# Longer runs for broadcast codes, six keys to a partition, and later loads in a routed attention kernel

## The chip, the core and the metric

The kernel runs on one core of a Trainium2 chip. The core has a matrix engine (TensorE, PE in the profile; its weight loads are PEld), a vector engine (VectorE, DVE), an activation engine (ScalarE, ACT), a general engine (GpSimd, POOL) and a queue engine (SyncE, SP), which here only issues DMA transfers. Each engine works through its own instructions in order, and waits on semaphores where it needs another one's result. Transfers run on 16 DMA engines, which all queues share. The metric is the device time of one execution in microseconds (us); lower is better.

## What is computed

Two blocks follow each other: an attention in which each query sees only the keys of its own cluster, and a two-layer network with the activation h - tanh(h).

```python
# attention: 4 batches, 8 heads, 768 positions, head size 64, 16 clusters
q_assign = np.argmax(np.einsum('bhsd,hcd->bhsc', q_n, c_n), axis=-1)
k_assign = np.argmax(np.einsum('bhsd,hcd->bhsc', k_n, c_n), axis=-1)
mask = q_assign[:, :, :, None] == k_assign[:, :, None, :]
scores = scale * np.matmul(q, k.transpose(0, 1, 3, 2))
scores = np.where(mask, scores, -1000000000.0)
...
attn = attn / (np.sum(attn, axis=-1, keepdims=True) + 1e-09)
return np.matmul(attn, v).astype(np.float32)
# network: 3072 tokens, width 512, inner width 2048
h = x @ w_in
g = h - np.tanh(h)
return (g @ w_out).astype(np.float32)
```

The n in q_n, k_n and c_n stands for normalised vectors. The order of the keys of a head plays no part in the result, so long as k and v have the same one.

## The kernel before

**Pairs and steps.** Two heads make a pair, and there are 16 pairs: four to a batch. Pairs 0 to 3 are batch 0. The attention of a pair has two halves of 384 queries, and a half has three steps of 2 x 128 keys. The list of steps (L1055) first has half 0 of pairs 0 to 3 (12 steps), then half 1 of pairs 0 to 3 (12 steps), and then pairs 4 to 15 with six steps each. One loop (L1204) goes through the steps and writes out, for each, the instructions of all engines in the order in which they are to run; nothing is reordered later. In a step, the scores of the following step are begun (`begin`, L473), the values of the present one are multiplied (`value`, L529), and a list of small jobs, `todo`, is spread between the matmuls of the network's work that fills the step.

**Codes and masks.** `load` (L317) fetches q and k of a pair on SP's queue; `turn` transposes them, on PE for batch 0 and on DVE in blocks of 32 for the others. `similar`, `turn_back`, `route` and `route_on` (L368 to L407) find the cluster of every query and key, as a number, the code. `publish` (L418) transposes the codes on PE, copies them to SBUF as bfloat16 (L427) and stores them to DRAM (L429), from where they are broadcast over partitions.

There are two ways to apply the mask. For half 0 of pairs 1 to 3 (the function `masked`), `spread_both` (L441) broadcasts the codes of queries and keys of each head to 64 partitions, into a tile named hot. `one_hot` (L452) turns them on DVE into a 0/1 row per cluster for the queries and a large negative number for the keys, in two instructions (L456, L460). A small matmul (L492) then adds the product to the scores before the exponential (L503). In all other halves, `spread` (L433) broadcasts the query codes to 128 partitions, into a tile named row, and `select` (L505) compares and multiplies on DVE (L513).

In `codes` a number stands at [partition, query or key, block of 128, head], and in DRAM in the order side, half, block, head, position. So one head's codes lie in runs of 128 numbers.

**When things are due.** `before` (L1059) yields the stages of a pair's preparation, and a table, `ready` (L1082), tells the step of each: for pairs of batch 0 the steps 0 to 4 after 3 (n - 2), for the others the steps -1, 0, 1 and 3 after a first step that is the pair before's first. The first stage of a pair n of batches 1 to 3 is its turn (of k; the turn of q has a place of its own, TURN_Q), and right behind it stands the load of pair n + 1:

```python
            def turns():
                turn(n, 1, nc.scalar)
                if rowwise(n):
                    turn(n, 0, nc.scalar)
                if n >= HP:
                    load(n + 1)
```

**The network.** The first half of batch 0 is multiplied plainly (L710, L726). From the second half on it is done with seven products in place of eight blocks. `up_items` (L881) gives a list of products for each of eight row blocks i, in the order 1, 2, 6, 7, 4, 5, 3. Products 6, 4 and 5 multiply differences of the input (the tile diff, made on DVE by `right_factors`, L879), the others the input itself. Their PSUM results (pu, L913) rotate through three buffers that other small results share, and DVE adds them (L908). Their weights come in as a stream from DRAM (`fetch_factors`, L833), two blocks ahead, in three buffers. The combined weights are made on DVE in steps 20 to 23 and stored by SP (L775). `start_without` (L950) takes a list of products and puts the first two of the second block ahead of the third of the first one; the half batch of batch 0 and the last batch use it.

**Queues.** SP issues nearly all transfers, in the order in which the program writes them. POOL issues the loads of the network's weights (raw, L218), which ACT and DVE then round (L149, L158, L161), as many pieces in each step as a table of paces says.

Of the kernel before, what the change touches and what calls it, by code (L numbers as in the profile page):

```python
# [30 lines left out]
F32 = mybir.dt.float32  # L31
# [8 lines left out]
P = 128  # L40
# [18 lines left out]
def kernel(  # L59
# [119 lines left out]
    def fast():  # L179
# [133 lines left out]
        def rowwise(n: int):  # L313

            return n < HP

        def load(n: int, what=(0, 1)):  # L317
            if n >= len(pairs):
                return
            b, p = pairs[n]  # L320
            for i in what:
                if i < 2:
                    pool, tag = (gp, "g") if b == 0 else (loads, f"x{i}")
                    shape = [P, NCH, 2, D] if rowwise(n) else [P, NBL, BL]
                    t = raw_qk[n, i] = pool.tile(shape, F32, name=f"x{i}", tag=tag)
                else:
                    pool = vp0 if n in (2, 3) else vp
                    t = vals[n] = pool.tile([P, 2, NCH, D], F32, name="vals")
                for h in range(2):
                    src = (q, k, v)[i][b, 2 * p + h]  # L330
                    if i == 2 or rowwise(n):
                        nc.sync.dma_start(
                            t[:, :, h] if i < 2 else t[:, h],
                            src.rearrange("(j p) d -> p j d", p=P),
                        )
                        continue
# [81 lines left out]
        def publish(n: int):  # L418

            sides = 2 if masked(n, 0) else 1  # L420
            G = HCH * 4 * sides
            ps = ps_f.tile([G, P], F32, name="pq", tag="f")
            nc.tensor.transpose(
                out=ps, in_=codes[n][:, 0:sides].rearrange("p i j h -> p (i j h)"), identity=ident
            )
            t = rtp.tile([G, P], BF16, name=f"qc{sides}")
            nc.vector.tensor_copy(out=t, in_=ps)  # L427
            q_codes[n] = dram.tile([sides, 2, HCH, 2, P], BF16, name=f"q_codes{sides}")
            nc.sync.dma_start(q_codes[n].rearrange("i a j h p -> (i a j h) p"), t)  # L429

        rows, hots = {}, {}

        def spread(n: int, half: int):  # L433

            t = rows[n, half] = rowp.tile([P, HCH, 2, P], BF16, name="row")
            nc.sync.dma_start(
                t.rearrange("p j h n -> p (j h n)"),
                q_codes[n][0, half].rearrange("j h n -> (j h n)").unsqueeze(0).to_broadcast([P, 2 * TB]),
            )

        def spread_both(n: int):  # L441

            t = hots[n] = gp.tile([P, 2, 2, TB], BF16, name="hot", tag="g")
            for h in range(2):
                nc.sync.dma_start(
                    t[h * D : h * D + D].rearrange("p i a (j n) -> p (i a j) n", n=P),
                    q_codes[n].rearrange("i a j h n -> h (i a j) n")[h].unsqueeze(0).to_broadcast(
                        [D, 2 * NCH, P]
                    ),
                )  # L450

# [53 lines left out]
        def select(n: int, half: int, j: int):  # L505

            if not masked(n, half):
# [3 lines left out]
                sc = e if summed(n, half) else scores.pop((n, half, j))  # L511
                for h in range(2):
                    nc.vector.scalar_tensor_tensor(  # L513
                        out=e[:, h].rearrange("p (j n) -> p j n", n=P), in0=rows[n, half][:, :, h],
                        scalar=codes[n][:, 1, j, h : h + 1],
                        in1=sc[:, h, 0:TB].rearrange("p (j n) -> p j n", n=P),
                        op0=ALU.is_equal, op1=ALU.mult,
                    )
# [685 lines left out]
        for at, (n, half, s) in enumerate(steps):  # L1204
# [370 lines left out]
```

## Time and profile before

| what | us |
| --- | --- |
| median of 3 runs | 964.34 (964.09 to 966.26) |
| the profiled execution | 965.51 |
| its span | 963.6 |
| TensorE busy | 944.9 |
| VectorE busy | 572.9 |
| GpSimd busy | 511.4 |
| ScalarE busy | 293.2 |

The span reaches from the first to the last instruction of the profiled execution. "Busy" is the time in which an engine executes, so that 944.9 us of 963.6 leave PE 18.7 us of idle time. The mean granted clock of PE was 0.996 of its full speed. On the 16 DMA engines, 139.84 MB moved in 175,723 packets, 127,332 of them under 512 bytes. A timeline shows an instruction's start, its duration, its engine, line and operation, the tiles as output<-input, and in brackets how long the engine was idle before it and who ended that. A line of waits tells who waited for whom, with the total, the number and the longest.

### The profile page before, as it was taken

What the parts mean: (1) busy time and instruction counts of PE and PEld (TensorE: products, weight loads), DVE (VectorE), ACT (ScalarE), POOL (GpSimd) and SP (SyncE); (2) the same over time, 40 slices, a digit from 0 to 9 for tenths busy, and PEclk for the clock granted to TensorE, in tenths of its full rate; (3) what the DMA queues carried; (4) which work ended last, traced back from release to release, by engine and by line L of the source; (5) the groups of instructions that cost most, each with busy time, mean ns of one, the idle gap of its engine ahead of it and who ended that gap; (6) DMA issues with size and microseconds to landing.
All of it is one profiled execution on the core that took longest, in us unless ns stands there. A gap on an engine that the chain in (4) does not pass through costs nothing.

```text
span 963.6 us, 16921 instructions
## 1 busy us (share of the span) xinstructions
PE 944.9 (98%) x6584; PEld 459.0 (48%) x6584; DVE 572.9 (59%) x1098; ACT 293.2 (30%) x453; POOL 511.4 (53%) x364
## 2 busy tenths in 40 slices
PE   8989999999999999999999999999999999999997
PEld 5423443345653333444455555444455555445664
DVE  7538587976775778657755558657654447443011
ACT  5556554224332232333322122332331211212000
POOL 1015344546675554687686444767797354567500
PEclk9989999999999999999999999999999999999999
DMA  8957455792745635473564748256344223323221
GB/s 201 192 138 166 142 137 140 230 267 99 185 128 159 171 115 141 150 185 115 169 186 152 190 150 214 92 165 181 102 146 145 86 89 105 102 91 131 106 105 36
DMA packets 175723, 139.84 MB, mean 145 GB/s; under 512 B 127332, under 2 KB 154388, under 8 KB 172948
## 3 DMA queue, kind: packets, MB, share of 16 engines
q1 hardware_dynamic: 169252, 117.15, 43.8%
q0 software_dynamic: 6240, 21.50, 6.9%
q8 instruction: 54, 0.88, 0.4%
q14 instruction: 33, 0.27, 0.1%
q10 hardware_dynamic: 144, 0.03, 0.0%
HBM read 117.48 MB, written 21.17 MB: 144 GB/s over the span
## 4 chain that ended last, share of the span: by engine, by line
PE 92%; DVE 4%; DMA 2%; issue 1%; ACT 1%; SPq 0%; DVEq 0%; ACTq 0%
PE pu L913 25%; PE pd L1009 23%; PE sc L481 14%; PE av L536 13%; PE o L726 8%; PE h L710 4%; DVE e L513 1%; PE sim L376 1%; DMA hot<-q_codes 1%; PE warm L302 1%; DMA stream<-up_factors 1%; PE den L597 1%; PE den L551 1%; PE den L570 1%; DVE diff L879 0%
## 5 line engine op out<-in xcount | busy, mean ns | idle before, releaser
L527 POOL TENSOR_TENSOR sum<-sum,e 128x768 f32<-128x768 f32 x112 | 207.5, 1852 | 86.9 <-DVE e L513 82.7
L513 DVE SCALAR_TENSOR_TENSOR e<-row,code,sc 128x384 f32<-128x384 bf16 x336 | 185.7, 607 | 61.8 <-ACT sc L503 48.3
L503 ACT ACTIVATE sc<-sc 128x768 f32<-128x768 f32 x168 | 125.8, 790 | 236.8 <-PE sc L481 219.5
L1009 PE MATMUL pd<-stream,G 128*64 128x256 f32 x1728 | 191.2, 379 | 0.0
L913 PE MATMUL pu<-xT,stream 128*64 128x384 f32 (+1 forms) x1024 | 159.9, 447 | 2.3 <-DMA stream<-up_factors 1.4
L1009 PEld LDWEIGHTS pd<-stream,G 128*64 128x64 f32 x1728 | 123.9, 137 | 66.9 <-issue 7.2
L481 PE MATMUL sc<-t,t 64*128 64x384 f32 x768 | 150.0, 509 | 0.3 <-ACT e L503 0.3
L536 PE MATMUL av<-e,vals 128*64 128x384 f32 x768 | 147.3, 503 | 0.9 <-DVE e L513 0.9
L982 POOL TENSOR_TENSOR G<-G,th 128x768 f32<-128x768 f32 (+1 forms) x51 | 87.2, 1723 | 77.7 <-ACT th L980 77.6
L913 PE MATMUL pu<-diff,stream 128*64 128x384 f32 (+1 forms) x768 | 121.2, 448 | 2.4 <-DVE diff L879 1.0
L913 PEld LDWEIGHTS pu<-xT,stream 128*64 128x64 f32 x1024 | 72.8, 137 | 77.0 <-issue 61.9
L481 PEld LDWEIGHTS sc<-t,t 64*128 64x128 f32 x768 | 66.2, 186 | 73.7 <-issue 35.8
L536 PEld LDWEIGHTS av<-e,vals 128*64 128x64 f32 x768 | 47.2, 137 | 86.7 <-issue 82.7
L523 POOL TENSOR_TENSOR sum<-e 128x768 f32<-128x768 f32 x28 | 52.6, 1880 | 64.6 <-DVE e L513 43.9
L726 PE MATMUL o<-w_out,g 128*64 128x512 f32 x384 | 86.1, 593 | 0.0
L980 ACT ACTIVATE th<-G 128x768 f32<-128x768 f32 (+1 forms) x51 | 40.9, 806 | 145.0 <-DVE G L908 140.2
L913 PEld LDWEIGHTS pu<-diff,stream 128*64 128x64 f32 x768 | 53.9, 137 | 59.6 <-issue 45.4
L908 DVE TENSOR_TENSOR G<-pu,u 128x384 f32<-128x384 f32 x72 | 39.6, 550 | 31.5 <-PE pu L913 31.4
L1020 DVE SCALAR_TENSOR_TENSOR c<-pd,du 128x256 f32<-128x256 f32 x36 | 15.1, 420 | 65.6 <-PE pd L1009 65.6
L726 PEld LDWEIGHTS o<-w_out,g 128*64 128x64 f32 x384 | 27.4, 137 | 50.1 <-issue 49.9
L1020 DVE SCALAR_TENSOR_TENSOR du<-pd,du 128x256 f32<-128x256 f32 x27 | 11.3, 420 | 59.1 <-PE pd L1009 59.1
L710 PE MATMUL h<-xT,w_in 128*64 128x384 f32 x256 | 42.8, 486 | 0.0
(136 smaller groups left out, 828.7 us busy)
## 6 DMA issues: line engine op xcount, KB each, us to landing
stream<-up_factors SPq DMA_DIRECT2D x32, 896.0 KB
stream<-down_factors SPq DMA_DIRECT2D x21, 1024.0 KB
raw<-in_moe_w_in_dram POOLq DMA_DIRECT2D x16, 512.0 KB, 5.3
raw<-in_moe_w_out_dram POOLq DMA_DIRECT2D x16, 512.0 KB, 4.8
again<-in_moe_w_in_dram SPq DMA_DIRECT2D x32, 256.0 KB
again<-in_moe_w_out_dram SPq DMA_DIRECT2D x32, 256.0 KB
vals<-in_v_dram SPq DMA_DIRECT2D x32, 192.0 KB
row<-q_codes SPq DMA_DIRECT2D x29, 192.0 KB
```

Of the source, the lines that this page charges most:

```text
L481: nc.tensor.matmul(sc[i][:, h, 0:TB], lhsT=turned[n, 1][r].rearrange("p a n -> p (a n)")[:, j * P : (j + 1) * P], rhs=turned[n, 0][r, half ...
L503: nc.scalar.activation(out=out, in_=sc[i][:, :, 0:TB], func=ACT.Exp, scale=SCALE)
L513: nc.vector.scalar_tensor_tensor(out=e[:, h].rearrange("p (j n) -> p j n", n=P), in0=rows[n, half][:, :, h], scalar=codes[n][:, 1, j, h : ...
L523: nc.gpsimd.tensor_tensor(out=s, in0=pair[0], in1=pair[1], op=ALU.add)
L527: nc.gpsimd.tensor_tensor(out=s, in0=s, in1=pair[i], op=ALU.add)
L536: nc.tensor.matmul(avs[n, half][h * D : h * D + D], lhsT=vals[n][:, h, j], rhs=e[i][:, h], start=(j == 0), stop=(j == NCH - 1),)
L710: nc.tensor.matmul(h[r], lhsT=w_in[i][:, c, o * P : (o + 1) * P][:, r], rhs=xT[c][:, half], start=(c == 0), stop=(c == CD - 1),)
L726: nc.tensor.matmul(acc[sub][r], lhsT=gs[f % HF][:, f // HF, sub * P : (sub + 1) * P][:, r], rhs=w_out[f // FQ][:, f % FQ], start=(f == seq ...
L913: nc.tensor.matmul(ps[r], lhsT=streams[base + i][:, c, k_, r], rhs=right[c], start=(c == 0), stop=(c == CH - 1),)
L980: nc.scalar.activation(out=th, in_=t, func=ACT.Tanh)
L982: nc.gpsimd.tensor_tensor(out=t, in0=t, in1=th, op=ALU.subtract)
L1009: nc.tensor.matmul(ps[r], lhsT=left(i)[:, r], rhs=t[:, i], start=(i == 0), stop=(i == HF - 1))
```

## The change

The diff has four parts.

1. For pairs 1 to 3 the codes are kept as [partition, head, query or key, block]. In DRAM they are ordered head, side, half, block, position. `spread_both` then broadcasts one run of 1,536 numbers per head in place of twelve of 128, and `spread` for half 1 of these pairs two runs of 384 in place of one of 768.
2. k and v of pairs 0 to 3 are loaded so that a partition holds six successive keys; before, it held every 128th. q stays as it was.
3. The load of pair n + 1 (for n from 4) moves from the turn of pair n to a place of its own, LOAD, two steps later, ahead of the step's list of jobs.
4. `start_without` is applied to the products of batches 1 and 2 too.

```diff
+                        order = "(p j) d -> p j d" if i and rowwise(n) else "(j p) d -> p j d"
                         nc.sync.dma_start(
-                            t[:, :, h] if i < 2 else t[:, h],
-                            src.rearrange("(j p) d -> p j d", p=P),
+                            t[:, :, h] if i < 2 else t[:, h], src.rearrange(order, p=P)
                         )
...
-            code = codes[n] = codep.tile([P, 2, NCH, 2], F32, name="code")
+            shape = [P, 2, 2, NCH] if masked(n, 0) else [P, 2, NCH, 2]
+            code = codes[n] = codep.tile(shape, F32, name="code")
+            if masked(n, 0):
+                nc.vector.reduce_max(
+                    out=code.rearrange("p h i j -> p (i j) h"),
+                    in_=top.rearrange("p (g h) c -> p g h c", h=2), axis=AX.X,
+                )
+                return
...
-            q_codes[n] = dram.tile([sides, 2, HCH, 2, P], BF16, name=f"q_codes{sides}")
-            nc.sync.dma_start(q_codes[n].rearrange("i a j h p -> (i a j h) p"), t)
+            shape = [2, HCH, 2, P] if sides == 1 else [2, sides, 2, HCH, P]
+            q_codes[n] = dram.tile(shape, BF16, name=f"q_codes{sides}")
+            order = "a j h p -> (a j h) p" if sides == 1 else "h i a j p -> (h i a j) p"
+            nc.sync.dma_start(q_codes[n].rearrange(order), t)
...
-            t = rows[n, half] = rowp.tile([P, HCH, 2, P], BF16, name="row")
+            t = rowp.tile([P, 2 * TB], BF16, name="row")
+            if masked(n, 0):
+                nc.sync.dma_start(
+                    t.rearrange("p (h n) -> p h n", h=2),
+                    q_codes[n][:, 0, half].rearrange("h j n -> h (j n)").unsqueeze(0).to_broadcast(
+                        [P, 2, TB]
+                    ),
+                )
+                rows[n, half] = t.rearrange("p (h j n) -> p h j n", h=2, j=HCH)
+                return
...
                 nc.sync.dma_start(
-                    t[h * D : h * D + D].rearrange("p i a (j n) -> p (i a j) n", n=P),
-                    q_codes[n].rearrange("i a j h n -> h (i a j) n")[h].unsqueeze(0).to_broadcast(
-                        [D, 2 * NCH, P]
+                    t[h * D : h * D + D].rearrange("p i a n -> p (i a n)"),
+                    q_codes[n][h].rearrange("i a j n -> (i a j n)").unsqueeze(0).to_broadcast(
+                        [D, 4 * TB]
                     ),
                 )
...
                 turn(n, 1, nc.scalar)
                 if rowwise(n):
                     turn(n, 0, nc.scalar)
-                if n >= HP:
-                    load(n + 1)
...
-        TURN_Q = 6
+        TURN_Q, LOAD = 6, 7
...
             if n >= HP:
+                ready.setdefault(first_step + 1, {})[LOAD] = lambda n=n: load(n + 1)
...
-            fills[2 * (b + 1) * HALF] = (lambda b=b: strassen_items(b), 2 * HALF)
+            fills[2 * (b + 1) * HALF] = (lambda b=b: start_without(strassen_items(b)), 2 * HALF)
...
+            if LOAD in stages:
+                stages[LOAD]()
             if TURN_Q in stages:
                 todo += [stages[0], stages[TURN_Q]]
```

`select` reads the code and the row tile through views that fit the new layout.

More of the change, by code (lines that the diff above doesn't have):

```diff
@@ L422, in publish @@
             ps = ps_f.tile([G, P], F32, name="pq", tag="f")
-            nc.tensor.transpose(
-                out=ps, in_=codes[n][:, 0:sides].rearrange("p i j h -> p (i j h)"), identity=ident
-            )
+            code = codes[n] if sides == 2 else codes[n][:, 0]
+            code = code.rearrange("p a b c -> p (a b c)" if sides == 2 else "p j h -> p (j h)")
+            nc.tensor.transpose(out=ps, in_=code, identity=ident)
             t = rtp.tile([G, P], BF16, name=f"qc{sides}")
             nc.vector.tensor_copy(out=t, in_=ps)
-            q_codes[n] = dram.tile([sides, 2, HCH, 2, P], BF16, name=f"q_codes{sides}")
-            nc.sync.dma_start(q_codes[n].rearrange("i a j h p -> (i a j h) p"), t)
+            shape = [2, HCH, 2, P] if sides == 1 else [2, sides, 2, HCH, P]
+            q_codes[n] = dram.tile(shape, BF16, name=f"q_codes{sides}")
+            order = "a j h p -> (a j h) p" if sides == 1 else "h i a j p -> (h i a j) p"
+            nc.sync.dma_start(q_codes[n].rearrange(order), t)
         rows, hots = {}, {}
         def spread(n: int, half: int):
-            t = rows[n, half] = rowp.tile([P, HCH, 2, P], BF16, name="row")
+            t = rowp.tile([P, 2 * TB], BF16, name="row")
[8 more added lines that the diff above has]
+                return
             nc.sync.dma_start(
-                t.rearrange("p j h n -> p (j h n)"),
-                q_codes[n][0, half].rearrange("j h n -> (j h n)").unsqueeze(0).to_broadcast([P, 2 * TB]),
+                t, q_codes[n][half].rearrange("j h n -> (j h n)").unsqueeze(0).to_broadcast([P, 2 * TB])
             )
+            rows[n, half] = t.rearrange("p (j h n) -> p h j n", h=2, j=HCH)
         def spread_both(n: int):
@@ L513, in select @@
                     nc.vector.scalar_tensor_tensor(
-                        out=e[:, h].rearrange("p (j n) -> p j n", n=P), in0=rows[n, half][:, :, h],
-                        scalar=codes[n][:, 1, j, h : h + 1],
+                        out=e[:, h].rearrange("p (j n) -> p j n", n=P), in0=rows[n, half][:, h],
+                        scalar=(
+                            codes[n][:, h, 1, j : j + 1] if masked(n, 0) else codes[n][:, 1, j, h : h + 1]
+                        ),
                         in1=sc[:, h, 0:TB].rearrange("p (j n) -> p j n", n=P),
```

## The prediction

> **What bounds the kernel now.** I read the busy table first: TensorE (PE) is busy 944.9 of 963.6 us, so an edit pays only where PE stands still, and at most 18.7 us in all. Of these, 6.1 lie after the last matmul and 1.3 before the first. The list of PE's waits says where most of the rest is (waiter, releaser: us in total, times, longest):
>
> ```profile
> PE sc L492 <- DVE hot L460: 4.6, 1, 4.6
> PE pu L913 <- DMA stream<-up_factors: 1.4, 1, 1.4
> PE pu L913 <- DVE diff L879: 1.0, 1, 1.0
> ```
>
> Then the timeline around the largest (start, us, engine, line, operation; in brackets the idle time before it and who ended it):
>
> ```profile
> 54.42 1.29 SPq L445 DMA_DIRECT2D hot<-q_codes  x2
> 57.18 1.56 PE L481 MATMUL sc<-t,t 64*128 64x384 f32 x8
> 62.60 0.42 DVE L456 TENSOR_SCALAR hot<-hot,mine_code 128x768 bf16<-128x768 bf16 x1 [6.91 <-DMA hot<-q_codes]
> 63.31 0.82 PE L492 MATMUL sc<-hot 64*128 64x384 bf16 x4 [4.57 <-DVE hot L460]
> 64.06 2.83 PE L536 MATMUL av<-e,vals 128*64 128x384 f32 x8
> 66.82 1.51 PE L551 MATMUL den<-e,ones 128*32 128x384 f32 x8
> 71.04 1.51 PE L536 MATMUL av<-e,vals 128*64 128x384 f32 x8
> 72.48 0.85 PE L551 MATMUL den<-e,ones 128*32 128x384 f32 x8
> ```
>
> The masks of pair 3 (tile hot) are issued at 54.42 and land just before 62.60; PE was free at 63.31 - 4.57 = 58.74. Behind the gap the same matmuls take nearly twice as long (L536 2.83 against 1.51), because the granted clock has fallen. The table by windows shows it in the seventh column, 0.66 of full speed (window, PE, PEld, DVE, ACT, POOL, clock, DMA share, GB/s):
>
> ```profile
> 60.00:70.00 10.00, 6.69 (x32) 2.24 (x32) 2.71 (x8) 3.60 (x6) 1.53 (x2) 0.66 0.49 119
> 70.00:80.00 10.00, 10.00 (x68) 3.54 (x64) 8.99 (x14) 8.38 (x13) 3.67 (x5) 1.00 1.08 211
> ```
>
> The clock records hold one stretch of 0.5, from 61.82 for 6.83 us, before the last one at 962.94. Extra time: L492 0.82 - 0.49, L536 2.83 - 1.51, L551 1.51 - 0.85, L481 1.73 - 1.56, together 2.48 us. So this one late transfer costs 4.57 + 2.48 = 7.05 us. Two later places complete the reading:
>
> ```profile
> 209.46 1.52 PE L913 MATMUL pu<-xT,stream 128*64 128x192 f32 x16 [1.38 <-DMA stream<-up_factors]
> 370.79 0.87 PE L913 MATMUL pu<-diff,stream 128*64 128x384 f32 x4 [1.04 <-DVE diff L879]
> 372.64 0.55 DVE L908 TENSOR_TENSOR G<-pu,s 128x384 f32<-128x384 f32 x1
> 373.25 1.51 PE L913 MATMUL pu<-diff,stream 128*64 128x384 f32 x8 [0.30 <-DVE G L908]
> ```
>
> **Part 1, codes kept head by head.** Each pair's hot is two DMAs of 64 partitions. Source runs grow from 128 bf16 (256 bytes) to 1,536 (3,072 bytes), so 2 x 64 x 12 = 1,536 packet records become 128, or 96 per DMA engine become 8. The packet records of before tell what that is worth. Pair 3's start at 57.0. About 660 pass in 0.75 us at 18 ns each; then the second of two weight loads (raw, 4,096-byte packets, another queue) arrives. From 59.0 to 59.75 there are 60 of raw's packets and 60 of hot's, turn by turn, and raw's take 164 to 192 ns each. Only after raw's last do the rest of hot's run, to 61.7; 0.9 us later DVE starts. So the small packets lose by their number, a turn each.
>
> After: a 3,072-byte packet is not in the trace. 1,536 bytes take 68 to 75 ns undisturbed, 7,168 take 272, so 117 to 150 ns; I take 0.14 us. Eight are 1.1 us alone; if every one waits one raw turn of 0.17, 2.5 us. Landing to DVE takes 0.5 us (row tile at 20.7 to 21.21) to 0.9, and DVE start to PE 0.71 (62.60 to 63.31). If the first packet still comes at 57.0, PE starts between 57.0 + 1.1 + 0.5 + 0.71 = 59.3 and 57.0 + 2.5 + 0.9 + 0.71 = 61.1, and 0.6 to 2.4 us of the wait stay.
>
> But it should start sooner. Pair 2's hot has DVE idle 5.72 us until 45.07. Its packets start at 40.0, so by the same prices it lands at 41.6 to 43.4. DVE then runs its chain to pair 3's code (3.5 us before) and two rounding steps 1.7 us or more earlier, and the copy of the codes (L427, 49.99) waits only for PE's transpose: 48.89 + 0.32 (that distance at 33.79 to 34.11) = 49.2. The q_codes store goes out 0.8 us sooner; it took 2.2 to 3.9 us to land (20.53 to 22.71, 50.52 to 54.42). So hot is issued by 49.7 + 3.9 = 53.6, and with 1.0 to 2.6 us from issue to first packet most of its 8 turns fall before 57.0. Landing before 58.0 leaves no wait. I take 0.3 us of it as left, nearer this case than 0.6 to 2.4. A remainder under 1.38 us costs no clock, since the gap at 209.46 had none. Gain 7.05 - 0.3 = 6.75 us (7.05 to 4.65).
>
> [...]
>
> What could be late next once PE runs 6.75 us sooner from 58.7 on? ACT, DVE and POOL wait for PE's results there and shift with it. DVE is busy 2.71 of 10 us in 60 to 70 and has room. den and list lie behind hot on the same queue and come sooner. The weights of L710 (84.64) are rounded well ahead: the second block's last piece by 64.4 us, needed after 95. So I count nothing.
>
> The rest of part 1: three row DMAs for half 1 go from 128 x 1,536 to 256 x 768 bytes; issued at 69.5, 79.4 and 112, used 10 us or more later: 0. Three maxima (L407, 0.55) write strided: if doubled, 1.65 us of DVE ahead of its waits for hot: 0. The selects (L513, 606 ns) read a contiguous row instead of a strided one, same size and types: 0.
>
> **Part 2, keys six to a partition.** The eight v transfers of pairs 0 to 3 go from 768 packets to 128; k's keep a destination in 256-byte pieces, so I count them as unchanged. The queue is full of 256-byte packets from 26 to 37 us (850 per us) and gets some 2 us shorter, but in PE's waits up to 85 us neither vals nor x stands: 0. Bounds +-0.3, by the gap of 0.93 at 21.90 whose row tile shares that queue.
>
> **Part 3, eight load DMAs two steps later, for pairs 5 to 15.** Each is some 6,144 packets of 128 bytes, 13 ns: 5 us, plus 4.3 us of SP issue (363.84 to 368.2) or 11.3 where the ring was full (201.70 to 213.0). Pair 5's moves from 139.8 behind the list of 150.5, where that queue is empty from 154 to 168, ahead of the factor stores that fill it from 170 to 207. Pair 6's moves from behind the first two stream fetches to behind the third and a row, and ahead of the fourth (218.17). The turn of a loaded pair comes four steps later, at least 26 us, against at most 18. So 0. Above: the 1.38 at 209.46; but 15 of that stream's 16 completions came by 208.1 and the last at 209.32, from an engine that still moved 7,168-byte packets until 208.7, and the load's are queued behind it. Below: see the slower rival.
>
> **Part 4, the third and fourth products moved ahead of the diffs in two batches.** PE then doesn't wait for diff at 370.79 (1.04). But the fifth product takes the PSUM buffer of the second (three in rotation), which DVE frees with the add of 372.64 to 373.19; DVE is busy without a break from 359.9. Four products are done at 373.2 either way, so 1.04 + 0.30 becomes one wait of about 1.8 and the net is 0 (gain at most 1.34, loss 0.4 for products that wait on DVE's longer queue).
>
> **Sum.** 6.75 + 0 + 0 + 0. Against the profiled execution: 965.51 (span 963.6 and 1.9 around it) - 6.75 = 958.8. The median of the runs is 964.34, 1.17 lower; measured like it, 957.6.
>
> **Rivals.** (B) Hot still starts at 57.0 behind raw's first load: the gain is 4.65 to 6.45, 957.9 to 959.7 (962.1 if a wait of 2.4 us lost the whole 2.48 of clock too; no row lies between 1.38 and 4.57). For it: the start at 57.0 is where raw's first burst ends. Against: 0.8 us of earlier codes. (C) The landing is late for another reason (store of q_codes, issue): a wait of 3 us and half the clock loss stay; gain 1.57 + 1.24 = 2.8, 961.5. Against: hot's own packets fill 57.0 to 61.7. (D) The 6.75 us are lost again later, at the factor stores or in rounding: 964. Against: PE has no wait on rounding at all. (E) Slower: the moved loads stand ahead of a stream fetch in the up stage. A fetch has about ten products, at 1.9 us each with attention between them 19 us, and needs 5.5 itself; load 4.3 + 5 leaves 4 us of room, but the 11.3 us issue leaves none. If each of 11 loads cost 1 us: 964.34 - 6.75 + 11 = 968.6; it decides from 0.6 us per load. Against: before, the same load stood ahead of a fetch at 363.84 and PE didn't wait.
>
> **Chances.** Forecast 0.70, B 0.13, C 0.05, D 0.05, E 0.07. 0.3% (2.9 us) is about what a measurement tells from no change. Forecast and B are faster, C splits: faster 0.84; same 0.08 (D and half of C); slower 0.08. Range: 956.2 (all 7.05 and 1.1 of parts 3 and 4) to 961.5 (C); the forecast's own is 956.9 to 958.6.
>
> **What would show it.** Right: no wait of L492 over 1 us, no clock under 1 before 960, hot in 128 packets, PE's L710 starting near 77.9 instead of 84.64, and the gaps near 203 and 366 of the old size. Wrong: hot landing after 58; a new wait on stream after a load; PE's busy sum changed by more than the 2.48.

## The result and the profile after

The changed kernel takes 958.41 us (median of 5 runs, 957.28 to 958.53); the kernel before, run beside it, 965.93 (5 runs, 964.09 to 969.11). The ratio is 0.9919, 95% interval 0.9897 to 0.9941: faster, by 0.8%. The forecast was 957.6 with a range of 956.2 to 961.5, from a median of 964.34, so a ratio of 0.9930. The time and the place of the gain were right. The cause was in good part not: part 2, which the prediction counted as nothing, gives about half of the gain by its own runs (0.48% of the 0.81%, with an interval of 0.30 to 0.67).

Line numbers after the change are higher: the scores are L499 (L481 before), the small mask matmul L510 (L492), the values L556 (L536), the broadcast of pair 3 L463 (L445), the DVE work on it L474 and L478 (L456, L460), the store of the codes L438 (L429), the diff and add lines L899 and L928 (L879, L908).

The list of PE's waits of the changed kernel (waiter, releaser: us in total, times, longest) has no line for hot any more:

```profile
PE pu L933 <- DVE G L928: 1.8, 1, 1.8
PE warm L302 <- DVE inverses L231: 1.3, 1, 1.3
PE av L556 <- DVE e L531: 1.3, 1, 1.3
PE pu L933 <- DMA stream<-up_factors: 1.1, 1, 1.1
```

The timeline of the changed kernel at the old gap (start, us, engine, line, operation, in brackets the idle time before it):

```profile
53.44 1.09 SPq L463 DMA_DIRECT2D hot<-q_codes  x2
54.40 0.53 POOL L218 DMA_DIRECT2D raw<-in_moe_w_in_dram  x1 [6.92 <-ACT rest L150]
55.71 0.53 POOL L218 DMA_DIRECT2D raw<-in_moe_w_in_dram  x1 [0.79 <-ACT rest L150]
57.55 1.56 PE L499 MATMUL sc<-t,t 64*128 64x384 f32 x8
58.27 0.42 DVE L474 TENSOR_SCALAR hot<-hot,mine_code 128x768 bf16<-128x768 bf16 x1 [2.19 <-DMA hot<-q_codes]
58.98 0.50 PE L510 MATMUL sc<-hot 64*128 64x384 bf16 x4
59.41 1.51 PE L556 MATMUL av<-e,vals 128*64 128x384 f32 x8
```

The broadcast is issued at 53.44 instead of 54.42, ahead of the raw load of 54.40 instead of behind it, and DVE has it at 58.27 instead of 62.60. The matmul at 58.98 follows the scores without a gap. It is just in time: DVE's second instruction ends at 58.93. The values behind it take 1.51 us, not 2.83. The table by windows shows the full clock in its seventh column (window, PE, PEld, DVE, ACT, POOL, clock, DMA share, GB/s):

```profile
50.00:60.00 10.00, 10.00 (x72) 3.90 (x70) 3.51 (x8) 7.49 (x11) 1.25 (x3) 1.00 0.49 158
60.00:70.00 10.00, 10.00 (x70) 3.47 (x70) 6.47 (x13) 8.56 (x15) 3.35 (x5) 1.00 0.68 190
```

Where PE stands can be compared step by step, by the start of each step's scores. The changed kernel is 6.62 us ahead at the first step behind the old gap (61.63 against 68.26); ahead of the gap it is 0.37 behind, so the gap itself gave 7.0. Then 0.4 is lost at 74.46, where the scores stall inside their record (1.96 us instead of 1.56), and 0.3 won at the stream's gap (1.13 instead of 1.38 us of idle time). Two jumps of 0.39 each come at steps 51 and 75, 0.34 is given back in the last third, and 6.9 remain: the span is 956.7 us against 963.6. PE is busy 941.8 us, 3.1 less; 2.48 are the clock; of the rest, the network's products (pu) take 0.9 us less, and the scores 0.5 more, 0.4 of it at 74.46. Packets fell from 175,723 to 166,764.

### The profile page after: what moved, and what is told of

Same layout as the page of the kernel before. It is cut to its first block, busy times and chain, and to the rows that moved or that the text cites. A ratio compares the mean times of both kernels' runs of the same rounds, so it can differ in the third digit from the quotient of the medians.

```text
span 956.7 us, 16942 instructions
## 1 busy us (share of the span) xinstructions
PE 941.8 (98%) x6584; PEld 458.6 (48%) x6584; DVE 571.2 (60%) x1098; ACT 292.6 (31%) x453; POOL 512.1 (54%) x364
## 4 chain that ended last, share of the span: by engine, by line
PE 92%; DVE 2%; DMA 1%; ACT 1%; issue 1%; SPq 0%; DVEq 0%; ACTq 0%
PE pu L933 26%; PE pd L1029 23%; PE sc L499 14%; PE av L556 13%; PE o L746 8%; PE h L730 4%; PE sim L376 1%; DMA stream<-up_factors 1%; PE den L571 1%; PE den L617 1%; DVE e L531 1%; PE den L590 1%; DVE diff L899 0%; PE pq L432 0%; DVE t L348 0%
## 5 line engine op out<-in xcount | busy, mean ns | idle before, releaser
L499 PE MATMUL sc<-t,t 64*128 64x384 f32 x768 | 150.2, 509 | 0.4 <-ACT e L521 0.3
L556 PE MATMUL av<-e,vals 128*64 128x384 f32 x768 | 145.9, 499 | 1.3 <-DVE e L531 1.3
L499 PEld LDWEIGHTS sc<-t,t 64*128 64x128 f32 x768 | 65.9, 186 | 73.8 <-issue 37.6
L556 PEld LDWEIGHTS av<-e,vals 128*64 128x64 f32 x768 | 46.9, 136 | 86.3 <-issue 82.0
L928 DVE TENSOR_TENSOR G<-pu,u 128x384 f32<-128x384 f32 x72 | 39.7, 552 | 32.9 <-PE pu L933 32.9
```

The source lines that it names most:

```text
L499: nc.tensor.matmul(sc[i][:, h, 0:TB], lhsT=turned[n, 1][r].rearrange("p a n -> p (a n)")[:, j * P : (j + 1) * P], rhs=turned[n, 0][r, half ...
L556: nc.tensor.matmul(avs[n, half][h * D : h * D + D], lhsT=vals[n][:, h, j], rhs=e[i][:, h], start=(j == 0), stop=(j == NCH - 1),)
```

## The experiments

For most kernels below, one row of this table is the main reading. Lead is the time from the issue of pair 3's broadcast to that of the first of the two raw loads (negative: the raw load came first; for hot_late both loads). The last column but one is the time from the issue to DVE's first work on hot.

| kernel | packets of the broadcast | pair 2's broadcast issued | pair 3's issued | lead | issue to DVE | PE's wait |
| --- | --- | --- | --- | --- | --- | --- |
| before | 256 B | 38.68 | 54.42 | -0.41 | 8.18 | 4.57 |
| part2_only | 256 B | 38.75 | 54.63 | -0.04 | 9.11 | 5.14 |
| parts234 | 256 B | 36.85 | 54.06 | 0.26 | 7.07 | 2.79 |
| pairs12_long | 256 B | 38.68 | 53.69 | 0.67 | 6.15 | 1.46 |
| raw_moved | 256 B | 38.74 | 54.75 | 6.1 | 4.57 | 1.13 |
| pair3_long | 3,072 B | 38.25 | 54.00 | -0.13 | 7.22 | 3.34 |
| part1_only | 3,072 B | 38.40 | 54.29 | 0.01 | 7.79 | 3.76 |
| parts12 | 3,072 B | 37.80 | 53.62 | 0.79 | 4.39 | 0 |
| after | 3,072 B | 36.75 | 53.44 | 0.96 | 4.83 | 0 |
| hot_late3 | 3,072 B | 36.58 | 52.49 | 2.34 | 4.04 | 0 |
| part1_raw_moved | 3,072 B | 37.96 | 53.73 | 5.5 | 3.96 | 0 |
| hot_late | 3,072 B | 37.88 | 57.64 | -3.2, -1.8 | 4.75 | 3.88 |

### Which part makes the gain

part1_only is the changed kernel with parts 2 to 4 undone:

```diff
-                        order = "(p j) d -> p j d" if i and rowwise(n) else "(j p) d -> p j d"
+                        order = "(j p) d -> p j d"
...
+                if n >= HP:
+                    load(n + 1)
...
-                ready.setdefault(first_step + 1, {})[LOAD] = lambda n=n: load(n + 1)
...
-            fills[2 * (b + 1) * HALF] = (lambda b=b: start_without(strassen_items(b)), 2 * HALF)
+            fills[2 * (b + 1) * HALF] = (lambda b=b: strassen_items(b), 2 * HALF)
```

> The kernel before with part 1 of the change alone (codes head by head, hot in runs of 3,072 bytes). My theory (the late hot of pair 3 is all of the gain): no wait of TensorE on hot, no clock below 1 before the end, scores of step 10 some 6.6 to 7.1 us earlier than before, ratio 0.992 to 0.994. Rival (the parts need each other, since the shorter v loads and the moved loads clear the queue that hot runs on): a wait of 2 us or more on hot stays and the ratio is above 0.996.

Measured: 963.17 us, ratio 0.9975 (0.9958 to 0.9993). The timeline of this kernel:

```profile
54.29 1.09 SPq L463 DMA_DIRECT2D hot<-q_codes  x2
54.30 0.53 POOL L218 DMA_DIRECT2D raw<-in_moe_w_in_dram  x1 [4.84 <-ACT rest L150]
62.08 0.42 DVE L474 TENSOR_SCALAR hot<-hot,mine_code 128x768 bf16<-128x768 bf16 x1 [6.09 <-DMA hot<-q_codes]
62.78 0.82 PE L510 MATMUL sc<-hot 64*128 64x384 bf16 x4 [3.76 <-DVE hot L478]
```

A twelfth of the packets, and hot is only 0.52 us earlier than before. That contradicts the prediction's reason: the number of hot's packets isn't the main thing that made it late. The broadcast and the raw load were issued within 0.01 us of each other. In the packet records (each has a start, a duration and a size) its 128 packets take from 55.78 to 60.86, with 186 of raw's among them; the same 128 of the changed kernel take from 54.67 to 57.41, with 48 among them.

parts234 is the other side, the changed kernel with its codes in the old order (256-byte runs):

```diff
-            shape = [P, 2, 2, NCH] if masked(n, 0) else [P, 2, NCH, 2]
+            shape = [P, 2, NCH, 2]
...
-            order = "a j h p -> (a j h) p" if sides == 1 else "h i a j p -> (h i a j) p"
+            order = "a j h p -> (a j h) p" if sides == 1 else "i a j h p -> (i a j h) p"
```

> The changed kernel with part 1 taken back: keys six to a partition, later loads, and the third and fourth products ahead. My theory: TensorE's wait on hot is back at 3.5 to 4.6 us with a stretch of half clock behind it, and the time is that of before less at most 1.5 us, ratio 0.998 to 1.000. Rival (part 2 empties the queue and hot comes in time without longer runs): the wait on hot is below 1 us and the ratio 0.993 or less.

Measured: 961.82 us, ratio 0.9964 (0.9944 to 0.9983). In the profiled execution the broadcast goes out 0.26 us ahead of the raw load and takes 7.07 us; the wait is 2.79, and its matmul takes 0.82 us, as long as before (0.50 in the changed kernel):

```profile
61.83 0.82 PE L525 MATMUL sc<-hot 64*128 64x384 bf16 x4 [2.79 <-DVE hot L493]
```

Parts that were to be worth nothing gave more than part 1. Steps 51 and 75 show jumps of 0.39 us each here, and part1_only and parts12 have none: those are part 4's, 0.8 us together.

Then part 1 was split by pairs: pair3_long has long runs for pair 3 alone, pairs12_long for pairs 1 and 2 (with parts 2 to 4 undone in both).

```diff
+        def longrun(n: int):
+            return n in (3,)
...
-            shape = [P, 2, 2, NCH] if masked(n, 0) else [P, 2, NCH, 2]
+            shape = [P, 2, 2, NCH] if longrun(n) else [P, 2, NCH, 2]
```

> The kernel before, with the longer runs for pair 3 alone; pairs 1 and 2 keep 1,536 packets of 256 bytes each. It tells the number of pair 3's own packets from the earlier codes that pairs 1 and 2 bring about. If the number alone does it: pair 3's hot is issued as before at 54.4, first packet near 57.0, DVE starts on it at 58.6 to 60.4, and 0.6 to 2.4 us of the wait of 4.57 stay. If the gain needs the earlier issue, more than 3 us stay. If the first packet isn't held back by the weights' load at all, the wait is 0.

> The kernel before, with the longer runs for pairs 1 and 2, and pair 3 as it was with 1,536 packets. If the earlier issue is what matters: pair 3's hot is issued by 53.6, its packets run before the weights' load of 55.3, and TensorE's wait falls below 1.5 us. If the number of pair 3's own packets is what matters: the issue is earlier by 0.8 us or more, but the packets still trade turns with the weights' load, and 2.5 us or more of the wait stay.

Measured, one execution each: 962.76 and 963.02 us. The timeline of pair3_long, and of pairs12_long:

```profile
61.92 0.50 PE L525 MATMUL sc<-hot 64*128 64x384 bf16 x4 [3.34 <-DVE hot L493]
62.35 1.51 PE L571 MATMUL av<-e,vals 128*64 128x384 f32 x8
```

```profile
53.69 1.33 SPq L471 DMA_DIRECT2D hot<-q_codes  x2
54.36 0.53 POOL L218 DMA_DIRECT2D raw<-in_moe_w_in_dram  x1 [5.21 <-ACT rest L150]
59.84 0.42 DVE L489 TENSOR_SCALAR hot<-hot,mine_code 128x768 bf16<-128x768 bf16 x1 [3.80 <-DMA hot<-q_codes]
60.54 0.50 PE L525 MATMUL sc<-hot 64*128 64x384 bf16 x4 [1.46 <-DVE hot L493]
```

pairs12_long leaves the late transfer's own 1,536 packets as they were, and its wait falls by more than where they became 128. What it changed is the time of the issue, 53.69, and with it the lead. From here on the theory was: what counts is how far ahead of the two raw loads the broadcast is issued, and everything that moves pair 2's and pair 3's codes forward helps. The expectations below call it Q.

### Parts 1 and 2, and part 2 alone

parts12 undoes parts 3 and 4 alone, by the last three edits of part1_only's diff. part2_only is the kernel before with one edit:

```diff
+                        order = "(p j) d -> p j d" if i and rowwise(n) else "(j p) d -> p j d"
                         nc.sync.dma_start(
-                            t[:, :, h] if i < 2 else t[:, h],
-                            src.rearrange("(j p) d -> p j d", p=P),
+                            t[:, :, h] if i < 2 else t[:, h], src.rearrange(order, p=P)
```

> Parts 1 and 2 of the change (codes head by head, keys six to a partition) without parts 3 and 4. Theory Q (both are needed, the pair-3 broadcast has to be issued about 0.9 us ahead of the raw load at 54.3, and parts 3 and 4 matter only for about 0.8 us in the third and fourth product): pair 2's broadcast issued near 36.8, pair 3's at 53.4 to 53.6, vector work on it at 58.3 to 58.8, no wait of the hot matmuls over 0.5 us, no half clock before the end, and a span of about 957.5 (after's 956.7 plus 0.8), time near 959.3. Rival L (part 3, the later loads, is what empties the queue): pair 2's broadcast still at 38.4, a wait of some 3.8 us on hot, time near 963.

> Part 2 alone (keys six to a partition), codes in 256-byte runs as before. Theory Q: pair 2's code store lands some 1.5 to 1.9 us sooner (its broadcast issued at 36.8 instead of 38.7), pair 3's broadcast is issued near 54.05 and the wait on hot is near 2.8 us, 1.5 to 2 less than before: about 2.3 us faster than before. The prediction's reckoning (part 2 is worth nothing, within 0.3): wait 4.6, time within 0.3 us of before.

Measured: parts12 960.28 us, ratio 0.9931 (0.9909 to 0.9953), wait 0. The timeline of parts12:

```profile
53.62 1.09 SPq L463 DMA_DIRECT2D hot<-q_codes  x2
54.41 0.53 POOL L218 DMA_DIRECT2D raw<-in_moe_w_in_dram  x1 [7.61 <-ACT rest L150]
58.01 0.42 DVE L474 TENSOR_SCALAR hot<-hot,mine_code 128x768 bf16<-128x768 bf16 x1 [1.93 <-DMA hot<-q_codes]
58.96 0.49 PE L510 MATMUL sc<-hot 64*128 64x384 bf16 x4
```

Without part 4's 0.8 us and with 1.0 lost in a wait on DVE at 75.55 (0.4 in the changed kernel), its span is 958.5. Part 3 isn't needed for any of this; it was not run alone.

part2_only: 962.48 us, ratio 0.9952 (0.9933 to 0.9970), so about 4.6 us by the ratio (3.5 by the medians, 962.48 against 966.01), more than expected; the prediction's nothing is out. But its profiled execution shows none of it. Its time is 965.24, the longest of ten from 958.83 on, and there the broadcast came last of all, 0.04 us behind the raw load, with the longest landing of all kernels:

```profile
54.59 0.53 POOL L218 DMA_DIRECT2D raw<-in_moe_w_in_dram  x1 [4.71 <-ACT rest L150]
54.63 1.28 SPq L471 DMA_DIRECT2D hot<-q_codes  x2
63.74 0.42 DVE L489 TENSOR_SCALAR hot<-hot,mine_code 128x768 bf16<-128x768 bf16 x1 [7.47 <-DMA hot<-q_codes]
```

So this profile speaks for the lead, and only the runs for part 2's size. Why pair 2's broadcast went out no sooner here than before (38.75) stands in the packet records. Of the 24 packets of pair 2's store of codes, 22 had passed by 36.71, and the last two came at 38.07. A packet of 16,384 bytes, on the queue that the profile lists as instruction, ran from 36.30 to 37.23; behind it six 1,536-byte packets of v and then the two followed one by one, among those of a raw load. In the changed kernel, where such a packet came only at 39.53, all 24 had passed by 36.10. In parts12 and hot_late one ended at 36.65 and 36.74, the last two of the 24 came at that moment, and pair 2's broadcast was 1.1 us later than in the changed kernel.

With part 1 or part 2 missing, ten runs lie 6.4 to 7.6 us apart; five of parts12 lie within 3.1, five of the changed kernel within 1.3, but ten of raw_moved, where the raw loads are out of the way, within 3.9. That fits a race between two issues that is won in some executions, but no second execution was profiled to show it.

### Is it the sharing with the raw loads, or the packets?

raw_moved is the kernel before with the two raw loads moved behind the broadcast, by the table of paces:

```diff
-        paces = dict(enumerate((0, 0, 1, 1, 1, 0, 2, 1, 2, 1, 1, 0, 3, 2, 2, 2, 2, 2, 2, 3, 2)))
+        paces = dict(enumerate((0, 0, 1, 1, 1, 0, 0, 3, 2, 1, 1, 0, 3, 2, 2, 2, 2, 2, 2, 3, 2)))
```

part1_raw_moved is part1_only with the same edit.

> The kernel before with one change: the seventh and eighth of the parts of work that fetch and split the raw expert weights are given to other steps (paces 2 and 1 become 0 and 3), so that the two raw loads issued at 54.0 and 55.3 come behind the pair-3 broadcast; codes stay in 1,536 packets of 256 B and keys in packets of 256 B. Theory Q (sharing with the raw loads is the cost, not the number of packets): the broadcast's packets end within about 2 us of their start, vector work on hot begins 3 to 4.5 us after the issue (57.5 to 59 instead of 62.6), the wait on hot falls below 1 us, and the kernel is 5 to 7 us faster than before unless the raw loads are missed later. Theory P (the number of packets is the cost): issue to vector work still 7 us or more, wait over 3 us.

> Part 1 (codes head by head: 128 packets of 3,072 B) with the raw loads behind the broadcast, as in raw_moved, where 1,536 packets of 256 B took 4.57 us from issue to vector work. Theory Q: unshared, the number of packets is worth at most 0.7 us (their own times, 1,536 x 19 ns against 128 x 135 ns over 16 queues, give 1.8 against 1.1): 3.8 to 4.6 us. The prediction's step (1.1 to 2.5 us by the number alone) would give 2.1 to 3.5 us.

Measured: raw_moved 962.10 us, ratio 0.9961 (0.9950 to 0.9972). The timeline of raw_moved:

```profile
54.75 1.28 SPq L471 DMA_DIRECT2D hot<-q_codes  x2
59.32 0.42 DVE L489 TENSOR_SCALAR hot<-hot,mine_code 128x768 bf16<-128x768 bf16 x1 [8.72 <-DMA hot<-q_codes]
60.03 0.50 PE L525 MATMUL sc<-hot 64*128 64x384 bf16 x4 [1.13 <-DVE hot L493]
60.85 0.74 POOL L218 DMA_DIRECT2D raw<-in_moe_w_in_dram  x1 [10.46 <-DVE w_in L158]
69.23 1.62 PE L514 MATMUL sc<-t,t 64*128 64x384 f32 x8 [0.97 <-ACT e L536]
```

The same 1,536 packets, issued 0.33 us later than before, reach DVE after 4.57 us instead of 8.18. So sharing costs these packets 3.6 us. The gain isn't kept whole: three raw loads now come in a row from 60.85 on, ACT rounds them later, and PE waits for ACT at 63.30 (0.55) and 69.23 (0.97).

part1_raw_moved, one execution: 960.39 us, span 958.5, no wait on hot. Its timeline:

```profile
53.73 1.09 SPq L463 DMA_DIRECT2D hot<-q_codes  x2
57.69 0.42 DVE L474 TENSOR_SCALAR hot<-hot,mine_code 128x768 bf16<-128x768 bf16 x1 [8.33 <-DMA hot<-q_codes]
58.45 0.49 PE L510 MATMUL sc<-hot 64*128 64x384 bf16 x4
```

Here 128 packets without company take 3.96 us. Against 4.57, the number of packets alone is worth 0.6 us; against part1_only's 7.79, sharing costs the long packets 3.8. In company the number may be worth more: with a lead of about zero, 7.2 to 7.8 us against 9.1, and at leads of 0.79 and 0.67, 4.39 against 6.15.

### A delayed broadcast

hot_late is the changed kernel with three small reads ahead of pair 3's broadcast, meant to take its lead away and leave the rest; hot_late3 repairs it. The diff of hot_late3:

```diff
             t = hots[n] = gp.tile([P, 2, 2, TB], BF16, name="hot", tag="g")
+            if n == HP - 1:
+                idle = rtp.tile([1, HCH, P], BF16, name="idle")
+                for j in range(HCH):
+                    nc.sync.dma_start(idle[:, j], q_codes[n][0, 0, 0, j].unsqueeze(0))
```

(In hot_late the three, of 384 numbers each, went one after the other into the same buffer, and so waited for each other. For a tile of its own for each, hot_late2, SBUF has no room, since a pool of 12 kb to a partition found 11.66 left, so it has no time.)

> The changed kernel with one thing added: three small reads of 768 B (codes of pair 3 into a tile that nobody reads) are issued ahead of pair 3's broadcast, so that it is issued some 1.0 us later, at about 54.4, together with the raw load instead of 1 us ahead of it. Theory Q (the lead over the raw loads decides): issue to vector work grows from 4.8 to 7 or 8 us, the work begins at 61.5 to 62.5, the wait on hot is 2.5 to 3.5 us: 1 us of delay costs about 3. Rival (long packets and a shorter queue are what took the wait away): the work begins 1 us later, at 59.3, and the wait on hot is 1 us or less.

> hot_late again, with three small reads of 256 B into parts of one tile that don't wait for each other. In hot_late they shared one buffer, each waited for the one before, and the broadcast came 4.2 us late instead of 1; it began behind the raw loads' bursts and took 4.75 us. Now it should be issued at 54.4 to 54.8, within 0.4 us of the raw load at 54.4. Theory Q (the closer to the raw loads' issue, the longer, up to 9 us): issue to vector work 6.5 to 8 us, work at 61 to 62.5, wait on hot 2 to 3.5 us, span 960 to 962. Rival (long packets and the shorter queue took the wait away, the lead doesn't matter): 4.4 to 4.8 us, work at 59.0 to 59.5, wait on hot under 1 us, span under 958.

Neither gave the lead of zero that was wanted. The timeline of hot_late:

```profile
53.68 3.92 SPq L464 DMA_DIRECT2D idle<-q_codes  x3
57.64 1.09 SPq L468 DMA_DIRECT2D hot<-q_codes  x2
62.39 0.42 DVE L479 TENSOR_SCALAR hot<-hot,mine_code 128x768 bf16<-128x768 bf16 x1 [6.21 <-DMA hot<-q_codes]
```

The broadcast came 4.2 us late, behind most of the raw packets, and took 4.75 us, about as in the changed kernel; wait 3.88, 962.94 us. And of hot_late3 (958.21 us, ratio 0.9914, 0.9892 to 0.9936):

```profile
50.33 0.31 SPq L438 DMA_DIRECT2D q_codes<-qc  x1
51.62 0.83 SPq L465 DMA_DIRECT2D idle<-q_codes  x3
52.49 1.09 SPq L467 DMA_DIRECT2D hot<-q_codes  x2
56.53 0.42 DVE L478 TENSOR_SCALAR hot<-hot,mine_code 128x768 bf16<-128x768 bf16 x1
```

The delay was eaten up: the store of the codes landed in 1.29 us here, against 3.55 in the profiled execution of the changed kernel (49.89 to 53.44), and the broadcast was issued 0.95 us sooner than there, not later. The packet records say why. The store is 24 packets of 256 B. In hot_late3 all 24 pass from 51.12 to 51.24. In the changed kernel 22 pass from 50.68 to 50.78 and the last two at 52.41. The broadcast, which reads what the store wrote, goes out at 53.44. What ran before these two is in the records as well: another 16,384-byte packet of the instruction queue, from 50.93 to 52.42, at whose end they start. In eight of the 14 profiled executions the last two packets of this store start within 0.02 us of the end of such a packet, and the transfer that waits for the store is issued 3.55 to 4.34 us behind the store's issue. In hot_late3 and diff_pool (below) all 24 packets had passed before it began, at 51.62 and 51.37, and that transfer is issued 1.29 and 1.81 us behind. So the lead hangs on the time of this fetch as well, at which no part of the change aims.

So the direct test of a delay of 1 us stays undone. The table speaks for the lead by other rows: at -0.13 and 0.01 the long packets take 7.2 to 7.8 us, at 0.79 and more 4.0 to 4.8. Those two rows have the longer queue of 256-byte packets of v, 15 us earlier, too.

### The price of the clock

fill_gap is the kernel before with matmuls in the gap:

```diff
+            if step == (HP - 1, 0, 0):
+                keep_warm(10)
             for i in range(2):
                 j = 2 * s + i
                 out = sc[i][:, :, 0:TB]
```

> The kernel before with ten dummy matmuls of 128x256 (the warm-up's) put into TensorE's order just ahead of the hot matmuls of pair 3; nothing else is changed. They fill about 2.5 to 3 us of the wait. If the half clock after the wait follows from the idle stretch and costs 2.5 us as the prediction has it, the clock stays at 1.00 behind the wait, the four hot matmuls take 0.49 instead of 0.82, and the span falls by 2 to 2.5 us. If the prediction's 2.5 us is no loss of its own, the span stays within 0.5 us.

Measured, one execution: span 961.7. The timeline of fill_gap:

```profile
59.31 4.58 PE L302 MATMUL warm<-inverses 128*128 128x256 f32 x20
63.83 0.50 PE L527 MATMUL sc<-hot 64*128 64x384 bf16 x4
64.26 1.51 PE L573 MATMUL av<-e,vals 128*64 128x384 f32 x8
```

Hot comes 0.52 us later than before (63.83 against 63.31), and still the next step's scores begin 1.78 us earlier (66.48 against 68.26). That is 2.3 us, and 0.17 more comes inside that step's scores (1.56 us against 1.73): the step behind begins 1.95 us earlier (71.31 against 73.26). So the half clock cost 0.52 + 1.95 = 2.47 us; the prediction had 2.48. The dummy matmuls took 4.6 us, not 2.5 to 3, so no idle time was left at all.

### A try to beat both

diff_pool is the changed kernel with the first column's diffs of the second batch on GpSimd:

```diff
+            engine = nc.gpsimd if (b, c) == (1, 0) else nc.vector
...
-                nc.vector.tensor_tensor(out=out, in0=u, in1=w, op=ALU.subtract)
+                engine.tensor_tensor(out=out, in0=u, in1=w, op=ALU.subtract)
```

> The changed kernel with the subtractions of the first column of the second batch's up factors moved from the vector engine to GpSimd, which is idle around 361.8 to 366.4; meant to beat both. If the wait of 1.84 us at 366.80 comes from the vector engine's queue of such work, it goes and the time falls by 1 to 1.8 us to about 957; if GpSimd's slower subtractions come late for their matmuls or hold GpSimd's next sum, the wait moves there and the time stays within 0.5 us or grows.

Measured: 959.43 us, ratio 0.9936 (0.9912 to 0.9960): no better than the change. The median hides two groups: three of the six runs take 957.7 to 957.8 us and three 961.1 to 962.1. The profiled one is of the first group (957.73), so what the others lost is not seen. Its timeline:

```profile
361.89 1.35 DVE L900 TENSOR_TENSOR xT<-xT 128x384 f32<-128x384 f32 x1
362.79 1.31 POOL L900 TENSOR_TENSOR xT<-xT 128x384 f32<-128x384 f32 x1
366.18 1.51 PE L934 MATMUL pu<-diff,stream 128*64 128x384 f32 x8 [2.50 <-DVE G L929]
```

DVE's subtractions, 0.55 us each in the changed kernel but for the first, take 1.35 to 1.52 in diff_pool, the first beside another instruction of GpSimd (358.63 to 360.00), the rest beside GpSimd's subtractions. So DVE's four last from 359.06 to 364.5, 5.4 us, where all eight lasted from 360.34 to 365.2, 4.9 us. The first subtraction of the changed kernel, 1.35 us, stands beside an instruction of GpSimd as well (359.91 to 361.28). PE reaches the place 1.3 us sooner here, 0.8 of it by a shorter wait on the stream, and waits 2.50 us instead of 1.84. None of the runs beats the changed kernel by more than its interval.

## Why the prediction was right, and where it was wrong

- **The bound and the size of the prize.** Right. 7.05 us hung on one late transfer: the wait of 4.57 is gone in the changed kernel, the half clock too, and fill_gap prices the clock at 2.47 us apart from the wait. The gap itself gave 7.0 us, of which 6.62 are left behind it; forecast were 6.75. The 0.3 us left as a wait became 0. (5.7 us lie after the last matmul, not 6.1; nothing rests on it. PE's busy sum fell by more than the 2.48, which the prediction named as a sign of being wrong; the difference is the products' and the scores', as said above.)
- **"So the small packets lose by their number, a turn each."** Wrong as the main cause. In part1_only the 128 packets still took 7.79 us; in raw_moved the 1,536 took 4.57. The turns with raw are real, but what decides is whether the raw loads are there at the time. The number alone is 0.6 us (4.57 against 3.96). The price of one packet was near: 121 ns by the median in hot_late3, 134 in the changed kernel and 188 among part1_only's many raw packets, taken as 0.14. (In its reading of before, about 660 of hot's packets pass in the first 1.0 us, not 0.75, and 29 of raw's still pass after 59.75.) With 128 packets in place of 1,536, part1_only still kept a wait of 3.76 us.
- **"So hot is issued by 49.7 + 3.9 = 53.6."** Right for the changed kernel (53.44), and this was the step that mattered. But it was derived from part 1 alone, by shorter packets of pair 2's hot. Part 1 alone gave 54.29. The store went out at 49.95 there instead of 49.7, and took 4.34 us, more than the upper end of 3.9. Even the changed kernel's 53.44 has chance in it: the instruction packet held the store up by some 1.6 us, and in diff_pool, where it came later, the broadcast went out at 51.90.
- **Part 2: "in PE's waits up to 85 us neither vals nor x stands: 0."** This is the step that failed. What stands in the same queue behind the packets of v is pair 2's store of codes, issued near 34.8. The timeline of the kernel before, and of the changed one:

```profile
35.09 0.50 SPq L429 DMA_DIRECT2D q_codes<-qc  x1
38.68 1.91 SPq L445 DMA_DIRECT2D hot<-q_codes  x2
```

```profile
34.79 0.32 SPq L438 DMA_DIRECT2D q_codes<-qc  x1
36.75 1.12 SPq L463 DMA_DIRECT2D hot<-q_codes  x2
```

  Before, 256-byte packets pass at 850 per us until 37.5, and the store lands after 3.59 us (35.09 to 38.68); in the changed kernel the queue is empty by 35.9, and it lands after 1.96 (34.79 to 36.75). The chain from there is the one that the prediction itself had described: pair 2's hot reaches DVE 2.5 us earlier (42.54 against 45.07), the raw load behind DVE's rounding goes out 2.5 us earlier (46.95 against 49.49), and pair 3's store finds it out of the way (packets at 50.7 instead of 52.3 to 53.6). The runs put part 2 alone at 0.48% (0.30 to 0.67) and part 1 alone at 0.25% (0.07 to 0.42). Together they are 0.73%, and both at once measured 0.69%. The way from part 2 to the gain is read from the changed kernel and from parts234, whose pair 2 broadcast goes out at 36.85; in part2_only's one profiled execution the instruction packet hid it.
- **Part 4: "1.04 + 0.30 becomes one wait of about 1.8 and the net is 0."** The wait is there as described, its size almost exact. The changed kernel's timeline:

```profile
366.80 1.51 PE L933 MATMUL pu<-diff,stream 128*64 128x384 f32 x8 [1.84 <-DVE G L928]
```

  The net there is 0, but two other places gain 0.39 us each, at the steps 51 and 75 behind it: a term of 0 that measured 0.8, within the bounds given (gain up to 1.34).
- **Part 3: 0.** No jump of PE's lead at any moved load, and the stream's gap stayed (1.13 us). The slower rival, loads ahead of a stream fetch, had no wait to show. The rows give the long issues of such loads, 11.3 us before (201.70) and 13.1 us in the changed kernel (197.07); that a full ring made them long was the author's reading, which no row shows.
- **The rivals.** Part 1 by itself is nearest to rival C in size (a wait of 3 us and half the clock loss stay, gain 2.8; part1_only's span is 2.4 shorter, its wait 3.76), but by the sharing with raw that rival B is about, and B gave it a gain of 4.65 at least. Rival D (the gain lost again later) is true for 0.4 us at 74.46 and 0.34 in the last third. That the forecast came out right is in part luck, because two errors met: part 1 was given part 2's work.

## What to carry to other kernels

Here a transfer's delay went with what stood in its queue when it was issued (pair 2's store of codes landed after 3.59 us behind 256-byte packets of v, after 1.96 behind fewer and longer ones) and with what other queues issued in the same microsecond (pair 3's broadcast took 8.18 us beside two raw loads, 4.57 without them), the packets of the instruction queue among them (pair 3's store took 3.55 us with one of 16,384 bytes between its packets, 1.29 with that one behind them); look at all of these in the packet records, and follow each store or broadcast upstream to the transfers that stand ahead of its own inputs, even when none of these appears in any engine's waits. Where a small urgent transfer and a bulk load are issued within a microsecond of each other, put the urgent one first by the order of the program, or move the bulk load, before its packets are reshaped: here the long packets at a lead of 0.79 us and more left no wait, the moved loads took 3.6 us off the 8.18, and the number of packets alone was worth 0.6. A kernel whose runs scatter by several us after a partial edit (here by 6.4 to 7.6) may have such a race that is only sometimes won; one profiled execution then doesn't stand for the others.

## What the runs showed of the hardware

- **The last two packets of a small store came behind a large packet of the instruction queue.** In the changed kernel, 22 of the store's 24 packets passed within 0.1 us and two came 1.6 us later, at the end of a 16,384-byte packet of the instruction queue that took 1.49 us; in hot_late3, where that packet came behind them, none did. The records don't name the DMA engine of a packet; that the two stood behind the large one on the same engine is inferred from the times, in eight executions.
- **Matmuls ran slower behind some of the waits, and not by the wait's length alone.** Behind waits of 2.79 (parts234), 3.76 (part1_only), 4.57 (before) and 5.14 us (part2_only) the four hot matmuls took 0.82 us; behind the wait of 3.34 in pair3_long they took 0.50, as without a wait (0.49 or 0.50), and the values behind them 1.51. The prediction had no row between 1.38 and 4.57 for this. How long this lasted differed too. The clock records of before hold one stretch of 0.5 ahead of 960, of 6.83 us, and the matmuls took 2.48 us more. (The stretches at full clock in before and the changed kernel are whole multiples of it: 54.61 and 894.29 us, 8 and 131 times, and 948.91, 139 times; no run shows why.) In parts234 and part1_only the hot matmuls and the values took 0.82 and 2.77, and 0.82 and 2.81, against 0.49 and 1.51, and den's matmuls were at 0.85 again, so about 1.6 us more. So the 2.48 us are the price of that one wait, confirmed by fill_gap (2.47); what sorts the waits was not shown.
- **DVE's subtractions took longer beside some work of GpSimd.** The same float32 subtractions of 128x384 took 0.55 or 0.56 us in the changed kernel with GpSimd idle (361.73 to 365.2), and 1.35 to 1.52 in diff_pool beside GpSimd's work. It is not so for all work: DVE's adds at 367.70 and 368.36 in the changed kernel took 0.56 beside GpSimd's sums (366.43 to 370.13).
